# Dealing the last weight sums behind evictions, a spare buffer for one copy, and five smaller moves in a retention + FFN kernel

## The chip, the cores and the metric

The kernel runs on one core of one Trainium2 chip. A core has five engines with a queue each: TensorE (PE, matrix products), VectorE (DVE), ScalarE (ACT), GpSimd (POOL) and SyncE (SP, which here only issues transfers). They run side by side and wait for each other through semaphores. SBUF is the working memory, PSUM [...] the memory that TensorE writes to; moving a result out of PSUM is called an eviction. The metric is the device time of one execution in microseconds, of which the median of several runs is taken.

## The reference

```
# retention: 8 batches, 8 heads, 576 positions, head size 64
scores = (q @ k^T) / sqrt(64)
out    = (scores * D[h]) @ v,   D[h][s, t] = gamma[h] ** (s - t) for s >= t, else 0
x      = out as 4608 tokens x 512
# multiplicative FFN, d_ff = 1024
a, b = x @ w1, x @ w2            # 512 x 1024 each
out  = ((a * b) @ w3) @ w_out    # 1024 x 1024, then 1024 x 512
```

The four weight matrices come as 8-byte floats and are turned into 4-byte floats on the chip.

## The kernel before

**Tokens.** Two batches are treated together, in four pairs. A pair's 576 positions are cut into five chunks (64, then four times 128) for the retention and into three blocks of 192 positions for the FFN; a block holds 384 tokens (two batches), and there are twelve blocks, counted by `m`. The counter `g` runs over the 20 chunks.

**Retention.** For a chunk, `load` fetches k, q, v; `scale` multiplies q and v by the decays (on VectorE, GpSimd or ScalarE); `front` transposes k and q on TensorE (tile `tp`) and ScalarE copies them out (`kT`, `qT`). Later chunks are loaded in 32-blocks and transposed by VectorE instead (`front_blocks`). `score` forms `sc` and VectorE masks it into `pm`; `state` adds to the running state `st`, which ScalarE copies to `sb`; `pv_state` and `pv` form `xps`, and the function that `pv` returns copies it into the block's `xT`.

**FFN, first four blocks (blocks 0 to 3).** `up` computes a and b for one block and one quarter `fp` of the columns with Strassen's seven products (L524). `strassen_tokens` makes the sums of token quarters that these need (L496), `strassen_weights` those of weight quarters (L149). After a product VectorE adds it to a partial sum (`plus`, L529), and behind each such addition `up` issues other work: some steps of the weight conversion (`convert`) and one entry each of the lists `aside` and `spread`. w3 and w_out are multiplied with each other once (`w3_mm`, L477), giving `w3o`; `down` then multiplies the tokens' a*b with `w3o`, again with seven products (L637, tile `po`).

**FFN, the other eight blocks.** Their products (`up2`, L1039) are two-level Strassen products over groups of two blocks. The weight forms for them are made in place in the weight tiles by `weight_forms` (six VectorE sums for each half of the columns and kind, L874), sent to DRAM (`kept`, L884 to L890), and fetched again one step ahead by `next_forms` into a ring of three buffers `ra` (L941), from POOL's queue. `token_forms` builds the sums of tokens as a list `pieces`, of which an entry is issued behind an addition of `down` when `spread` is empty.

**The switch at chunk `g` = 9.** `open_first` takes over the memory of the first half of the weights: it issues the remaining sums of the second half (`spread.extend(weight_forms(1, True))`, `flush()`), whose transfers to `kept` follow them on SP's queue. Then come a product with w_out for blocks 2 and 3, and `open_second`, which closes the PSUM pool `acc` with seven buffers and opens one with five, and a third product with w_out for block 3. In these, `down` copies its first product out of PSUM by ScalarE into `first` (L669): this lies in the output tile `ot` until the ring is in use, and from then on in a spare piece of the ring. `ot` has one buffer, so it is free only when the stores of the product before it have landed.

**What sets the order.** Nothing is scheduled by a planner: each engine takes its instructions in the order in which the Python code issues them. `keep_busy(n)` issues n products of the unit matrix with itself, which no one reads.

Of the kernel before, what the change touches and what calls it, by code (L numbers as in the profile page):

```python
# [19 lines left out]
def kernel(  # L20
# [13 lines left out]
    nc = tc.nc  # L34
# [449 lines left out]
    def has_x(i, n):  # L484
        return any(starts[c] + sizes[c] >= (n + 1) * TB and ("x", i * NC + c) in live for c in range(NC))

    def strassen_tokens(i, n, engine=nc.gpsimd):

        m = every.index((i, n))
        x = live["xT", m]  # L490
        B = [[x[:, 2 * r:2 * r + 2, b, :] for b in range(2)] for r in range(2)]
        T = [(t_first if m == 1 and j == 2 else ffn).tile(
            [P, 2, TB], F32, tag="T", name="T", bufs=1 if m == 1 and j == 2 else 5) for j in range(3)]

        def tt(out, in0, in1, op=ALU.subtract):
            engine.tensor_tensor(out=out, in0=in0, in1=in1, op=op)  # L496

        live["B", i, n] = {"B11": B[0][0], "B21": B[1][0], "B22": B[1][1], "T3": B[0][1],
                           "T1": T[0], "T2": T[1], "-T4": T[2]}
        tt(B[0][1], B[1][1], B[0][1])  # L500
        tt(T[1], B[0][1], B[0][0], ALU.add)
        yield
        tt(T[0], B[1][1], T[1])
        tt(T[2], B[1][0], T[1])
        yield

    def up(i, n, fp, conv=0, tail=True, first=False):
        m = every.index((i, n))
        while ("S", fp) not in live:
            assert go_on() is None  # L510
        if ("B", i, n) not in live:
            list(strassen_tokens(i, n))
        if fp == 0:
            live["ab", i, n] = (pools["ab3"] if m == 2 else ffn).tile([P, 2 * KF, TB], F32, tag="ab", name="ab")
        ab = live["ab", i, n]

        def product(ps, a, b):
            a, b = A(fp, a), live["B", i, n][b]
            new = ps is None
            if new:  # L520
                ps = acc.tile([P, 2, TB], F32, tag="acc", name="up")
            for w in range(2):
                for r in range(2):
                    nc.tensor.matmul(ps[:, w, :], a[:, w, r, :], b[:, r, :], start=(new and w == r == 0),  # L524
                                     stop=(w == r == 1), skip_group_check=True)
            return ps

        def plus(ps, to, sb):
            nc.vector.tensor_add(c[:, to], ps, c[:, sb])  # L529
            convert(conv.pop(0) if isinstance(conv, list) else conv)  # L530
            for extra in (aside, spread):
                if extra:
                    extra.pop(0)()


        c = ffn.tile([P, 4, 2, TB], F32, tag="c", name="c", bufs=1)
        p1 = product(None, "A11", "B11")
        nc.scalar.copy(c[:, 0], p1)

        convert(owed.pop() if owed else 0)  # L540
        if first:

            p7 = product(None, "S3", "T3")
            product(p1, "A12", "B21")
            aside.pop(0)()
        plus(product(None, "S2", "T2"), 1, 0)
        plus(p7 if first else product(None, "S3", "T3"), 2, 1)
        p5 = product(None, "S1", "T1")
        plus(p5, 3, 2)
        plus(product(None, "A22", "-T4"), 2, 2)  # L550
        if not first:
            product(p1, "A12", "B21")
        nc.scalar.copy(c[:, 0], p1)
        product(p5, "S4", "B22")
        plus(p5, 1, 1)

        if fp == NQ - 1 and m < NB - 1 and has_x(*every[m + 1]) and ("B", *every[m + 1]) not in live:
            list(strassen_tokens(*every[m + 1]))
        nc.vector.tensor_mul(ab[:, 4 * fp:4 * fp + 4, :], c[:, :, 0, :], c[:, :, 1, :])
        if tail:  # L560
            convert(conv)
# [63 lines left out]
    def down(x, y, then=None, last=False):  # L625
        a, done, left = pair_of(x, y)
        second = "first" in live
        ahead(x, y)
        while len(done) < (1 if second else 3):
            aside.pop(0)()  # L630
        ps = {}
        ot = pools["ot"].tile([P, 2, 2, DM // 2], F32, tag="ot", name="ot")

        def product(nm, A, B, on=None):
            ps[nm] = ps[on] if on else acc.tile([P, DM // 2], F32, tag="acc", name="po")
            for f in range(NP):
                nc.tensor.matmul(ps[nm], a[A][:, f, :], live["W"][B][:, f, :], start=(f == 0 and not on),  # L637
                                 stop=(f == NP - 1), skip_group_check=True)

        def plus(nm, to, sb):  # L640
            nc.vector.tensor_add(ot[:, to[0], to[1]], ps[nm], ot[:, sb[0], sb[1]])
            if spread:
                spread.pop(0)()
            elif pieces:
                pieces.pop(0)()
            if second and aside and nm != 3:
                aside.pop(0)()

        def put(m, t, row, half=slice(0, 2)):

            i, n = every[m]
            r0 = t * P
            while r0 < (t + 1) * P:
                b = r0 // TB
                e = min((b + 1) * TB, (t + 1) * P)
                r = (2 * i + b) * S + n * TB + r0 - b * TB
                stores.append((out[r:r + e - r0, half.start * DM // 2:half.stop * DM // 2],
                               ot[r0 - t * P:e - t * P, row, half].rearrange("p h d -> p (h d)")))
                r0 = e
            if not keep_stores and not second:  # L660
                store()

        C11, C12, C21, C22 = (0, 0), (0, 1), (1, 0), (1, 1)
        product(1, "A11", "B11")
        first = ot[:, 0, 0]
        if second and steps[0]:
            first = live["first"].pop(0)
            live["first"].append(first)
        nc.scalar.copy(first, ps[1])  # L669
        if second:  # L670
            store()
            finish()
        product(7, "S3", "T3")
        if second:
            multiply()
        while len(done) < 3:
            aside.pop(0)()
        if then:
            ahead(*then)
        product(2, "A12", "B21", on=1)  # L680
        nc.vector.tensor_tensor(out=a["S4"], in0=a["A12"], in1=a["S2"], op=ALU.subtract)
        product(6, "S2", "T2")
        nc.vector.tensor_add(ot[:, 0, 1], ps[6], first)
        nc.scalar.copy(ot[:, 0, 0], ps[2])
        early = second or last or g >= 2 * NC - 1
        if early:
            put(*x, 0, slice(0, 1))
            store()
        plus(7, C21, C12)
        product(5, "S1", "T1")  # L690
        plus(5, C22, C21)
        product(4, "A22", "-T4")
        plus(4, C21, C21)
        put(*y, 1)
        if second:
            store()
        product(3, "S4", "B22", on=5)
        while aside and not early:
            aside.pop(0)()
        plus(3, C12, C12)  # L700
        put(*x, 0, slice(1 if early else 0, 2))
        if last:
            store()
        while aside:
            aside.pop(0)()
# [38 lines left out]
    pv_state(1)  # L744
    convert_up_to(3)
    convert(2)
    state(1)
    load(3, "kq")
    weight_sums = strassen_weights(0)
    next(weight_sums)  # L750
    pv(1)()
    keep_busy(4)
    load(3, "v")
    load_block()
    convert_up_to(4)
# [2 lines left out]
    next(weight_sums)  # L758
    list(token_sums)
    list(weight_sums)  # L760
    aside.append(lambda: scale(2, "q", True))
    scale(2, "v")
    up(0, 0, 0, conv=[0, 0, 2, 2, 2], tail=False, first=True)
    front(2)
    convert(1)
    score(2)
    state(2)
# [143 lines left out]
    def open_first():  # L911
# [3 lines left out]
        ring.append(ra[:, :FORM])  # L915
        next_forms(nc.sync)
        spread.extend(weight_forms(1, True))
        flush()
        free.extend(cs[:, j] for j in range(2))
        live["T2"] = ra[:, FORM:].rearrange("p (s k c t) -> p s k c t", s=2, k=3, c=2)  # L920
        live["E"] = ffn.tile([P, 4, 2, TB], F32, tag="c", name="e", bufs=1).rearrange("p (e r) b t -> p e r b t", e=2)
# [22 lines left out]
    def token_forms(gr):  # L944
# [35 lines left out]
        def inner(k):  # L980
# [5 lines left out]
            for i, nm in enumerate(("T1", "T2") if k != 2 else ("-T4",)):  # L986
                part = [y[:, i] if k != 2 else y for y in (b11, b21, b22, b12, *u)]
                forms[nm] = dict(zip(names, part))

        pieces.extend([first, lambda: tt(b12, b22, b12), lambda: tt(E[:, 1], b12, b11, ALU.add),  # L990
                       lambda: tt(E[:, 0], b22, E[:, 1])])
        pieces.extend([lambda: pair(1), lambda: pair(0), lambda: pair(2), outer, lambda: inner(slice(0, 2)),
                       lambda: inner(2)] if gr else
                      [outer, lambda: pair(1), lambda: pair(0), lambda: pair(2), lambda: inner(slice(0, 2)),
                       lambda: inner(2)])

    behind, results, sums2 = [], [], {}

    def finish():
        while behind:  # L1000
            behind.pop(0)()
# [140 lines left out]
    for g in first_pair:  # L1142
# [9 lines left out]
        if in_blocks[g + 1]:  # L1152
            scale_blocks(g + 1)
            work(n - 1)
            aside.extend(lambda nm=nm: front_blocks(g + 1, nm) for nm in "kq")
            work(1)
            while aside:
                aside.pop(0)()
            half = 0
# [25 lines left out]
    pv(g)()  # L1185
    load(g + 2, "v", nc.scalar)
    load(g + 2, "k")
    scale(g + 1, "v")
    open_first()
    token_forms(0)  # L1190

# [105 lines left out]
```

## Time and profile before

| what | value |
|---|---|
| median of three runs | 838.39 us (836.72 to 839.96) |
| the profiled execution's own time | 944.19 us |
| its span, first to last instruction | 942.5 us |
| mean granted TensorE clock in it | 0.846 |
| busy: PE, DVE, ACT, POOL | 931.7, 545.4, 289.7, 224.4 us |
| chain that ended last | PE 95%, DMA 3%, SP's queue 1% |
| products with w_out, L637 | 26% of the chain |
| products of `up`, L524; of `up2`, L1039 | 18%; 31% (18% and 13%) |
| clock granted from 10 to 15 us / from 30 us on | 0.50 / 0.85 |

The profile shows one execution, and that one took 12.6% longer than the median. Each matrix product of 4-byte floats stands in it as two instructions. "Busy" for PE is modelled: it runs to a modelled end of each product, so a PE that is busy throughout is not necessarily at its peak. A line of the timeline gives the start and the duration of a run of equal instructions, the engine, the source line, the operation, the tiles with their shapes and, in brackets, how long the engine stood idle before it and what released it.

### The profile page before, as it was taken

The numbers are of one execution on the slowest core, as the hardware profiler recorded it, in microseconds if no ns is written. First come the engines' busy times: TensorE is split into PE (matmuls) and PEld (weight loads), VectorE is DVE, ScalarE is ACT, GpSimd is POOL, SyncE is SP. The second block draws the span as 40 slices with busy tenths as digits, with TensorE's granted clock in tenths as the row PEclk, the third lists the DMA queues.
The fourth block names the chain that finished last, engine by engine and source line by source line (L and its number), as shares of the span: only waits on it lengthen the run. The fifth ranks groups of instructions, "written<-read, shape, count | busy, mean of one in ns | idle before, by whom it ended". The sixth has DMA issues, their size and how long they took to land.

```text
span 942.5 us, 15780 instructions
## 1 busy us (share of the span) xinstructions
PE 931.7 (99%) x6101; PEld 818.4 (87%) x6101; DVE 545.4 (58%) x957; ACT 289.7 (31%) x601; POOL 224.4 (24%) x249
## 2 busy tenths in 40 slices
PE   8999999999999999899999999999999999999998
PEld 7999999533888998689999789998789998799976
DVE  4888888970544467644557643657545555535542
ACT  4776454560111111044343023331033320033200
POOL 1100010002003172015536015463016250044500
PEclk7888888888888888888888888888888888888888
DMA  9992543426045475967675146868245352135311
GB/s 187 225 222 74 83 122 98 133 62 99 1 86 111 74 224 197 319 173 194 170 193 154 41 88 207 215 192 160 57 116 192 119 184 73 40 131 187 118 29 40
DMA packets 197868, 126.96 MB, mean 135 GB/s; under 512 B 157848, under 2 KB 179608, under 8 KB 197792
## 3 DMA queue, kind: packets, MB, share of 16 engines
q1 hardware_dynamic: 167520, 50.14, 26.4%
q0 software_dynamic: 11632, 62.79, 20.4%
q10 hardware_dynamic: 18640, 13.02, 5.0%
q8 instruction: 48, 0.79, 0.4%
q14 instruction: 28, 0.23, 0.1%
HBM read 103.62 MB, written 22.28 MB: 134 GB/s over the span
## 4 chain that ended last, share of the span: by engine, by line
PE 95%; DMA 3%; SPq 1%; ACT 0%; POOL 0%; issue 0%; DVE 0%; ACTq 0%
PE po L637 26%; PE up L524 18%; PE up L1039 18%; PE seed L1039 13%; PE ps L477 7%; PE xps L299 4%; PE sc L233 4%; PE xps L274 2%; PE st L255 2%; PE tp L218 1%; DMA ld_v<-in_v_dram 1%; DMA kept<-wA 1%; DMA ld_q<-in_q_dram 1%; DMA out_dram<-ot 1%; SPq L93 0%; SPq L342 0%
## 5 line engine op out<-in xcount | busy, mean ns | idle before, releaser
L637 PE MATMUL po<-w3o,ab 128*128 128x256 f32 x552 | 145.0, 426 | 2.8 <-ACT ot L669 2.2
L637 PEld LDWEIGHTS po<-w3o,ab 128*128 128x128 f32 x552 | 109.4, 200 | 32.5 <-ACT ot L669 2.7
L1044 POOL TENSOR_TENSOR cc<-cc 128x384 f32<-128x384 f32 x112 | 109.3, 1002 | 5.2 <-ACT cc L1062 3.7
L1051 DVE TENSOR_TENSOR cc<-seed,cc 128x384 f32<-128x384 f32 x88 | 49.0, 557 | 91.9 <-PE seed L1039 85.4
L941 POOL DMA_DIRECT2D ra<-kept x53 | 30.0, 566 | 243.5 <-PE seed L1039 181.1
L1039 PE MATMUL up<-xT,ra 128*128 128x192 f32 x384 | 83.7, 360 | 0.0
L529 DVE TENSOR_TENSOR c<-up,c 128x384 f32<-128x384 f32 x80 | 44.0, 551 | 64.9 <-PE up L524 64.4
L524 PE MATMUL up<-xT,wA 128*128 128x192 f32 x384 | 80.5, 360 | 0.0
L637 PE MATMUL po<-wB,forms 128*128 128x256 f32 x288 | 75.8, 425 | 0.0
L524 PEld LDWEIGHTS up<-xT,wA 128*128 128x128 f32 x384 | 72.0, 197 | 1.4 <-issue 0.6
L1051 DVE TENSOR_TENSOR cc<-up,cc 128x384 f32<-128x384 f32 x88 | 48.5, 551 | 42.5 <-PE up L1039 39.8
L1039 PEld LDWEIGHTS up<-xT,ra 128*128 128x128 f32 x384 | 72.0, 198 | 1.3 <-issue 0.4
L637 PEld LDWEIGHTS po<-wB,forms 128*128 128x128 f32 x288 | 57.8, 201 | 15.2
L236 DVE TENSOR_TENSOR pm<-sc,mask 128x512 f32<-128x512 f32 (+1 forms) x80 | 45.4, 627 | 41.2 <-PE sc L233 41.1
L477 PE MATMUL ps<-wo,w3T 128*128 128x512 f32 x128 | 64.4, 673 | 0.0
L1058 ACT COPY seed<-up 128x384 f32<-128x384 f32 x56 | 25.9, 463 | 121.1 <-PE up L1039 118.5
L1039 PE MATMUL up<-ra 128*128 128x192 f32 x288 | 62.5, 359 | 0.0
L477 PEld LDWEIGHTS ps<-wo,w3T 128*128 128x128 f32 x128 | 25.5, 199 | 38.1 <-issue 37.8
L1039 PE MATMUL seed<-e,ra 128*128 128x192 f32 x256 | 57.4, 361 | 0.0
L1039 PEld LDWEIGHTS up<-ra 128*128 128x128 f32 x288 | 54.6, 198 | 0.2
L524 PE MATMUL up<-T,wS 128*128 128x192 f32 x256 | 53.5, 359 | 0.0
L181 POOL TENSOR_TENSOR bl_q<-bl_q,gqs 128x512 f32<-128x512 f32 (+1 forms) x26 | 27.9, 1093 | 103.3 <-DMA bl_q<-in_q_dram 101.3
(126 smaller groups left out, 1550.9 us busy)
## 6 DMA issues: line engine op xcount, KB each, us to landing
ra<-kept POOLq DMA_DIRECT2D x53, 896.0 KB, 4.9
raw<-in_moe_w_dram SPq DMA_DIRECT2D x72, 128.0 KB, 3.1
out_dram<-ot ACTq DMA_DIRECT2D x54, 128.0 KB, 2.3
bl_q<-in_q_dram SPq DMA_DIRECT2D x192, 32.0 KB, 3.0
bl_k<-in_k_dram SPq DMA_DIRECT2D x136, 32.0 KB, 3.0
raw<-in_moe_w_dram SPq DMA_DIRECT2D x16, 256.0 KB, 6.3
ld_k<-in_k_dram SPq DMA_DIRECT2D x8, 512.0 KB, 5.9
raw<-in_moe_w_out_dram SPq DMA_DIRECT2D x32, 128.0 KB, 2.7
```

Source lines behind the costliest of these rows:

```text
L181: nc.gpsimd.tensor_tensor(out=part, in0=part, in1=gqs[:, :, n0:n0 + n].unsqueeze(3).to_broadcast([P, NP, n, BL]), op=ALU.mult)
L233: nc.tensor.matmul(sc[j][:sz, p, :sz], kT[hs, b, p, :sz], qT[hs, b, p, :sz], start=True, stop=True)
L236: nc.vector.tensor_mul(pm[:sz, b, j, :, :sz], sc[j][:sz, :, :sz], mask[:sz, :sz].unsqueeze(1).to_broadcast([sz, NP, sz]))
L299: nc.tensor.matmul(banks[r][heads[half], b, n, :sz], vs[:sz, b * H + 2 * p + j, :], pm[:sz, b, j, p, :sz], start=(c == 0 and m == 0), stop ...
L477: nc.tensor.matmul(ps, live["w3T", ft][:, g, :], live["wo"][:, g, :], start=(g == 0), stop=(g == KF - 1))
L524: nc.tensor.matmul(ps[:, w, :], a[:, w, r, :], b[:, r, :], start=(new and w == r == 0), stop=(w == r == 1), skip_group_check=True)
L529: nc.vector.tensor_add(c[:, to], ps, c[:, sb])
L637: nc.tensor.matmul(ps[nm], a[A][:, f, :], live["W"][B][:, f, :], start=(f == 0 and not on), stop=(f == NP - 1), skip_group_check=True)
L941: engine.dma_start(ring[n % 3], kept[n % 14 // 7][nm])
L1039: nc.tensor.matmul(ps[:, w, :], weight_of(slot, a, w), B[b], start=(new and w == 0), stop=True, skip_group_check=True)
L1044: nc.gpsimd.tensor_tensor(out=o, in0=o, in1=i, op=ALU.add)
L1051: nc.vector.tensor_add(c[:, j], ps, with_add[:, j])
```

## The change

There are seven edits.

1. **Start.** `state(1)` is issued after `pv(1)` and not before it, and `keep_busy(4)` after it becomes `keep_busy(1)`. The transposes of chunk 2 (`front(2)`) move from behind the first `up` into it: those of k behind its third addition, those of q behind its fourth (two empty entries of `aside` stand ahead of them).
2. **Sums of the third block of tokens.** In the `up` for block 1 and the last quarter they are issued on VectorE, one behind each of the first four additions, in place of GpSimd at its end.
3. **Last weight sums.** `open_first` no longer flushes: the three pairs of sums and the transfers stay in `spread` and are issued behind the four additions of the product with w_out of blocks 2 and 3. The token sums of the first group wait until `spread` is empty, and are issued two at a time behind the additions of the product after it.
4. **First copy.** In that next product, `first` lies in the tile `cs` (name `cc`) which `open_first` laid into the first weight half's memory, and no longer in `ot`.
5. **Scaling of v** for chunk 10: on ScalarE, as eight instructions, no longer as one on GpSimd.
6. **Forms.** `down` may issue `next_forms` behind its first copy, so that one transfer per group leaves POOL's queue during a product with w_out and not with the first step of the next group.
7. **Order of VectorE's work.** `front_blocks` for q before k, with an empty place between; and for the later groups the outer token sums before the pairs.

```diff
-    def strassen_tokens(i, n, engine=nc.gpsimd):
+    def strassen_tokens(i, n, engine=nc.gpsimd, singly=False):
...
         tt(B[0][1], B[1][1], B[0][1])
+        if singly:
+            yield
         tt(T[1], B[0][1], B[0][0], ALU.add)
         yield
         tt(T[0], B[1][1], T[1])
+        if singly:
+            yield
         tt(T[2], B[1][0], T[1])
...
+        sums = ()
+        if fp == NQ - 1 and m < NB - 1 and has_x(*every[m + 1]) and ("B", *every[m + 1]) not in live:
+            sums = strassen_tokens(*every[m + 1], nc.vector, True)
+            aside.extend([lambda: next(sums)] * 4)
...
-        if fp == NQ - 1 and m < NB - 1 and has_x(*every[m + 1]) and ("B", *every[m + 1]) not in live:
-            list(strassen_tokens(*every[m + 1]))
+        list(sums)
...
-        if second and steps[0]:
+        if second and not steps[0]:
+            first = live["spare"]
+        elif second:
             first = live["first"].pop(0)
             live["first"].append(first)
         nc.scalar.copy(first, ps[1])
         if second:
             store()
             finish()
+            if steps[0] and sent[0] < steps[0] + 3:
+                next_forms()
...
-    state(1)
     load(3, "kq")
...
     pv(1)()
-    keep_busy(4)
+    state(1)
+    keep_busy(1)
...
-    aside.append(lambda: scale(2, "q", True))
+    aside.extend([lambda: scale(2, "q", True), lambda: None, lambda: None,
+                  lambda: front(2, "k"), lambda: front(2, "q")])
     scale(2, "v")
     up(0, 0, 0, conv=[0, 0, 2, 2, 2], tail=False, first=True)
-    front(2)
...
         spread.extend(weight_forms(1, True))
-        flush()
+        live["spare"] = cs[:, 1].rearrange("p a b t -> p (a b t)")[:, :DM // 2]
...
-        pieces.extend([first, lambda: tt(b12, b22, b12), lambda: tt(E[:, 1], b12, b11, ALU.add),
-                       lambda: tt(E[:, 0], b22, E[:, 1])])
-        pieces.extend([lambda: pair(1), lambda: pair(0), lambda: pair(2), outer, lambda: inner(slice(0, 2)),
-                       lambda: inner(2)] if gr else
-                      [outer, lambda: pair(1), lambda: pair(0), lambda: pair(2), lambda: inner(slice(0, 2)),
-                       lambda: inner(2)])
+        parts = [first, lambda: tt(b12, b22, b12), lambda: tt(E[:, 1], b12, b11, ALU.add),
+                 lambda: tt(E[:, 0], b22, E[:, 1]), outer, lambda: pair(1), lambda: pair(0), lambda: pair(2),
+                 lambda: inner(slice(0, 2)), lambda: inner(2)]
+        if not gr:
+
+            parts = [lambda two=parts[j:j + 2]: [f() for f in two] for j in range(0, 8, 2)] + parts[8:]
+        pieces.extend(parts)
...
-            aside.extend(lambda nm=nm: front_blocks(g + 1, nm) for nm in "kq")
+            aside.extend([lambda: front_blocks(g + 1, "q"), lambda: None, lambda: front_blocks(g + 1, "k")])
...
-    scale(g + 1, "v")
+    scale(g + 1, "v", True)
     open_first()
     token_forms(0)
```

## The prediction

> **What bounds the kernel now.** I read the page first, its busy row and its chain (95% PE), and then measured the starts of successive products against each other.
>
> ```profile
> span 942.5 us, 15780 instructions
> PE 931.7 (99%) x6101; PEld 818.4 (87%) x6101; DVE 545.4 (58%) x957; ACT 289.7 (31%) x601; POOL 224.4 (24%) x249
> ```
>
> TensorE is the bound. Its busy time is modelled, so I took starts: a product of `up` (eight records) starts every 1.50 us, and from 412 us to the end no group of PE's instructions has more than 0.1 us of idle before it. Only idle time of PE can be won. The idle rows and the timeline leave three places. First the start, where a first product waits for a copy:
>
> ```profile
> 25.35 1.21 PE L255 MATMUL st<-ld_v,ld_k 128*64 128x64 f32 x32 [0.28 <-POOL ld_v L204]
> 26.38 2.18 PE L299 MATMUL xps<-pm,ld_v 128*64 128x128 f32 x32
> 28.49 1.27 PE L131 MATMUL idle<-ident 128*128 128x128 f32 x8
> ```
>
> ```profile
> 27.43 0.56 ACT L259 COPY sb<-st 128x512 f32<-128x512 f32 x1
> 28.36 1.07 ACT L306 COPY xT<-xps 128x512 f32<-128x512 f32 x2 [0.36 <-PE xps L299]
> ```
>
> `up` starts at 29.58, when that second copy is out (29.43). Second, a wait of TensorE for VectorE, while GpSimd makes the sums of the third block of tokens:
>
> ```profile
> 122.56 1.50 DVE L413 SCALAR_TENSOR_TENSOR e<-raw,e 128x512 int32<-128x512 int32 x1
> ...
> 125.17 1.09 DVE L399 TENSOR_SCALAR m<-raw 128x512 int32<-128x512 int32 x1
> ...
> 126.66 1.30 DVE L402 SCALAR_TENSOR_TENSOR m<-raw,m 128x512 f32<-128x512 uint32 x1
> ```
>
> ```profile
> 128.48 1.74 PE L524 MATMUL up<-xT,wS 128*128 128x192 f32 x8 [0.65 <-DVE c L529]
> ```
>
> Elsewhere these three take 0.68, 0.42 and 0.69 us. Third, the switch of pools:
>
> ```profile
> 391.07 4.25 PE L637 MATMUL po<-w3o,ab 128*128 128x256 f32 x16 [0.52 <-DVE ot L641]
> 397.49 3.19 PE L637 MATMUL po<-w3o,ab 128*128 128x256 f32 x8 [2.16 <-ACT ot L669]
> ```
>
> ```profile
> 397.06 0.37 ACT L669 COPY ot<-po 128x256 f32<-128x256 f32 x1 [11.59 <-DMA kept<-wA]
> ```
>
> ```profile
> 395.00:400.00 5.00, 2.84 (x9) 2.06 (x8) 0.00 (x0) 0.37 (x1) 0.00 (x0) 0.73 1.11 372
> ```
>
> The last is the view by windows: the seventh figure (0.73) is the granted clock, 0.85 around it. So after the wait the clock is lower, here and from 400 to 405 (0.73 again): 10 x 0.12 / 0.85 = 1.4 us more.
>
> **What the skill says.** The Trainium skill, "SBUF — State Buffer", section "Who interferes with whom", has VectorE and GpSimd share a pair of ports: an instruction of VectorE with two SBUF inputs blocks against a GpSimd instruction that reads SBUF. The trace agrees for the sums: 0.82 + 0.67 + 0.61 = 2.1 us lost over three instructions beside GpSimd's four. (The middle one has one tensor input, which that sentence does not cover.) "TensorE: Matmul & The Clock Gate", section "What's actually happening", halves the clock after a window of some 3.4 us with too little work, and the window runs freely. The trace agrees: 1.4 us are what 3.4 us at 0.5 in place of 0.85 cost, after an idle time of only 2.2 us. So it needn't trip in every execution.
>
> **The time frame.** The profiled execution took 944.19 us against a median of 838.39, a ratio of 0.89. At a clock of 0.846 TensorE's work would shrink to 797 us at full clock, so the runs shown are probably at a faster clock, with more waiting than the profile has. Waits on copies, transfers and VectorE don't shrink. I make the sum in the profile's frame and then look at what 0.89 does to PE's share.
>
> **Part by part.**
>
> *Start.* Before, `st` holds PE from 25.35 to 26.38 and `xps` till 28.5. After, `xps` comes first: v is ready at 25.3 and the last mask product of VectorE at 25.43 (22.95 + 2.48), so it ends near 27.5. ScalarE is free at 27.5 and has no `sb` copy ahead: copies out at 28.55. `st` ends at 28.5, one idle product adds 0.3: `up` at 28.7, 0.85 earlier. The second product needs VectorE's token sum, issued at 29.68 in a stream without a gap since 25.35, ready at 30.23; the first takes 1.5 us, so it just fits. Three idle products (0.3 us each) were filling, not work. The moved transposes cost PE the same 1.0 us each, and their copies come earlier on ScalarE, in the place of an eviction whose user is VectorE at 42. Gain 0.85; nothing if VectorE's stream holds it back later, 1.2 if the 0.18 us before the next scores goes too.
>
> *Third block.* Added to VectorE: four sums at 0.5 us (0.55, 0.56, 1.02 for two, L496 at 29.7) = 2.1 us, in the `up` from 130.06 to 140.60, where its idle times are 0.17 + 0.19 + 2.11 = 2.5 us: hidden. If that cover is gone they cost up to 2.1 us. Taken away: the 2.1 us of blocking just before. The wait of 0.65 us falls. Their user starts at 140.6; the last sum is issued behind the fourth addition, near 137. Gain 0.65; ends -1.0 and +2.1.
>
> *Last weight sums.* Before, six sums ran in a row (377.02 to 383.04) while products went on, hiding all. After, they sit behind the additions of a product, as the pairs before them already do:
>
> ```profile
> 367.63 0.42 DVE L641 TENSOR_TENSOR ot<-po,ot 128x256 f32<-128x256 f32 x1
> 367.97 1.22 DVE L874 TENSOR_TENSOR wA<-wA 128x1024 f32<-128x1024 f32 x1
> 369.10 0.95 DVE L874 TENSOR_TENSOR wS<-wS 128x768 f32<-128x768 f32 x1
> 369.97 0.42 DVE L641 TENSOR_TENSOR ot<-po,ot 128x256 f32<-128x256 f32 x1
> ```
>
> Every addition then takes 2.34 us against 2.03 of a product. That product began at 358.79; its last addition ended at 375.06, 16.27 us on, while PE needs 14.24. The product with the same pattern is now the one in front of `open_second`, whose first product waits for just that last addition. The wait there grows from 0.67 (start to start) to some 2.05 us, with all of PE's queue behind it: a new loss of 1.4 us.
>
> *First copy.* With `cc` it no longer waits for the stores of the product before; `cc` needs the transfers out of the first half's sums, issued by 383. The wait of 2.35 us (start to start) goes: the next writers of `ot`, VectorE's L683 and ScalarE's L684, come some 6 us after the stores' issue, which took 5.7 to land. Behind L684 stand a store and the scaling of q (2.44 us), whose transposes start 8 us later. Net at the switch 3.0 before, 2.05 after: gain 0.95. The lowered clock may stay, as one wait of 2 us is much like the one that brought it: I take half of 1.4. Together 1.65; ends 0 and 2.4.
>
> *Transfers.* SP's sends for the second half stood at 388.18; they now follow the third pair, near 392.2. Queued behind them: the next fetch into the ring (402.62, then 406.6), landing in about 5.3, so 412 at the usual time, 415 at the slowest (8.2); its step starts near 416. ScalarE's own fetch (410.81) waits for the same sends. Taken at nothing; it is the loss of the second rival.
>
> *v on ScalarE.* Eight at 0.305 us = 2.44 ahead of the copy of the first product, which then ends near 380.0; its user starts at 380.37. Hidden, by 0.4; at the faster clock a loss up to 0.2. GpSimd's 1.9 us were on nobody's path.
>
> *Forms, order of transposes, order of sums.* PE has no idle in these stretches. A fetch needs 4.9 us, and even before it was issued two steps of 5.3 us ahead; its 0.57 us on POOL now stand before `scale_blocks`, whose user is a chunk away. VectorE is busy about 23 of 40 us there. Nothing; ends -0.5 and +0.5.
>
> *Sum.* 0.85 + 0.65 + 1.65 = 3.15 of 942.5 (0.33%). At 0.89, the start gives some 0.7; at the switch products of 1.8 us make the new wait 2.7 and the old ones 3.5, 0.8 gained. So about 2.9 us off 838.4: 835.5.
>
> **The rivals.** *Larger gain.* From 40 to 200 us VectorE is busy 136.7 of 160 us; at a faster clock PE would need 142, and VectorE is nearly the bound. Then whatever unblocks it counts fully: 1.2 + 2.1, with the switch at 0.95 and a clock that no longer drops, 1.4: 5.65, 832.7. For it: the waits that 838 must contain. Against: four sums are added where 2.1 us are freed.
>
> *A late fetch, slower.* The transfer engines are full (a share of 1.0 to 1.2 from 375 to 400 us). I have the sends landed at 406.6; from 410.7 on the fetch behind them (5.3 us) is later than its step at 416, and ScalarE stands at its own fetch with the first evictions of the next stage behind it. Sends at 414 and the slowest fetch (8.2) make PE stand 6 us, and the clock drops (1.4); less the 3 gained: 843. Against: four us of slack.
>
> *No effect.* VectorE's stream absorbs the start, the clock drops as before: 838.
>
> **Numbers.** Forecast 0.36, no effect 0.11 (both within 0.5%, 4.2 us, about what a measurement of this kernel can tell from no change), larger gain 0.34, slower 0.19. The forecast's own range is 834 to 837.5; 830 to 842 takes in most of the larger gain and part of the loss.
>
> **What would show it.** `up` at 28.7; no wait for VectorE near 128 and L399, L402, L413 at usual lengths; at the switch one wait of 2 us for L648 (the addition, renumbered), none for the first copy; the clock there. Wrong if PE waits on `ra` after the switch, or if the gain lies in the later groups.

## The result, and the profile after

| | median, us | ratio to before (95% interval) |
|---|---|---|
| before | 839.34 (835.90 to 843.75) | 1 |
| after | 840.27 (836.12 to 843.99) | 1.0005 (0.9989 to 1.0022) |

The change makes no difference that the measurement can tell: +0.4 us, between -0.9 and +1.8. The forecast was 835.5. The prediction read a profile of before at a mean clock of 0.846, and after's is at 0.998, so times are compared below only with a second profile of before, at 0.994 (span 834.6 us), called "before, second profile".

The page of after, its busy row:

```profile
span 839.2 us, 15778 instructions
PE 819.8 (98%) x6095; PEld 738.9 (88%) x6095; DVE 542.3 (65%) x961; ACT 291.9 (35%) x609; POOL 216.6 (26%) x244
```

TensorE is busy 820 us and not 932; what the change can win or lose is in the 19 us beside that, and in the clock. The timeline of after, the three places that the prediction named. First the start:

```profile
28.09 1.47 PE L528 MATMUL up<-xT,wA 128*128 128x192 f32 x8
30.35 1.86 PE L528 MATMUL up<-xT,wA 128*128 128x192 f32 x10 [0.80 <-DVE xT L496]
...
54.94 1.38 PE L528 MATMUL up<-T,wS 128*128 128x192 f32 x7 [1.22 <-ACT e L395]
```

In before's second profile the first two of these read:

```profile
29.29 1.47 PE L524 MATMUL up<-xT,wA 128*128 128x192 f32 x8
30.96 2.84 PE L524 MATMUL up<-xT,wA 128*128 128x192 f32 x16 [0.21 <-DVE xT L496]
```

`up` starts early as forecast, but its second product waits 0.80 us for VectorE's token sum, as it does for 0.21 us in before. Ahead of the edit, at the first scores, after is 0.62 us earlier already (21.74 against 22.36). The first product is 1.20 us earlier, so the edit won some 0.6; the token sum (29.66 against 30.27) and the second product are 0.61 earlier, so nothing of it is left there. At 54.94 one product waits 1.22 us, where before's waits 0.65. (ScalarE is named there, but the sum of weights that this product reads is made by VectorE from 54.11 to 54.80, the second of four in a row without a gap: VectorE is what is full.) Second, near 118 us, no wait of over 0.3 us is left. Third, the switch:

```profile
350.34 5.45 PE L644 MATMUL po<-w3o,ab 128*128 128x256 f32 x24 [2.68 <-DVE ot L648]
...
352.37 0.37 ACT L678 COPY cc<-po 128x256 f32<-128x256 f32 x1 [9.14 <-PE po L644]
```

The addition (L641 of before) is late by 2.68 us, the figure that the prediction has for a faster clock. The first copy waits only for its product. So far this is as forecast. The surprise stands 24 us later, in the first steps of `up2`. First TensorE, then ScalarE, then SP's queue:

```profile
369.78 0.81 PE L1051 MATMUL up<-xT,ra 128*128 128x192 f32 x4
374.67 0.92 PE L1051 MATMUL up<-xT,ra 128*128 128x192 f32 x4 [4.08 <-ACT cc L1074]
```

```profile
368.51 0.46 ACT L1070 COPY seed<-up 128x384 f32<-128x384 f32 x1 [2.61 <-PE up L1051]
373.76 0.34 ACTq L723 DMA_DIRECT2D out_dram<-ot  x1
374.14 0.48 ACT L1074 COPY cc<-up 128x384 f32<-128x384 f32 x1 [5.17 <-DMA bl_q<-in_q_dram]
```

```profile
362.80 0.34 SPq L952 DMA_DIRECT2D ra<-kept  x1
363.19 0.43 SPq L93 DMA_DIRECT2D ld_q<-in_q_dram  x1
364.01 14.43 SPq L171 DMA_DIRECT2D bl_q<-in_q_dram  x13
```

After the copy of `seed` (L1070) ScalarE's next instruction is the issue of a store of the output tile (L723). It goes out at 373.76, 4.8 us later, and the copy into `cc` that TensorE needs is behind it. What releases ScalarE is the landing of a block load of q, which has nothing to do with the output. After the wait the clock is low; the view by windows, whose seventh figure is the granted clock:

```profile
376.00:380.00 4.00, 4.00 (x16) 4.00 (x16) 2.52 (x5) 1.57 (x5) 0.00 (x0) 0.61 0.41 64
```

Why a load of q holds back a store is in the trace, which names the semaphore that each transfer counts up when it lands. In after the 591 transfers of SP's and ScalarE's queues use eight of these counters, handed out in turn. In the 510 cases where the trace has the landing of a counter's last user, none of the next users was issued before it. The store's counter is semaphore 102, which the first of the block loads of q has too: that load has landed at 373.68, the wait of ScalarE's queue for 102 ends at 373.72, and the store goes out at 373.76. Which transfer had the counter last depends on the transfers of both queues in between. (The fetches into the ring at the switch leave from these two queues, and not from POOL's.) For this store:

```
kernel                       its counter was last used by
before, second profile       the fetch ra<-kept on SP's queue, landed 1.2 us before the store's turn
first copy alone             the same fetch, landed when ScalarE had stood 2.6 us at the store
changed                      the first of sixteen block loads bl_q on SP's queue
sums in a row; switch alone  an earlier store of the output, landed 2.5 and 0.7 us before its turn
```

The Trainium skill, "DMA: Bandwidth & Descriptors", section "Why a DMA increments its semaphore by 16 and not by 1", says why a program would wait so: with two transfers in flight on one semaphore, a count can be reached before the first has fully landed. It advises a semaphore for each slot in flight. No run here tries two transfers on one counter; that a store waits for the landing of an unrelated transfer is what the trace shows, 4.8 us long.

### The profile page after: what moved, and what is told of

Read it like the earlier page. It is cut to its first block, busy times and chain, and to the rows that moved or that the text cites. A ratio compares the mean times of both kernels' runs of the same rounds, so it can differ in the third digit from the quotient of the medians.

```text
span 839.2 us, 15778 instructions
## 1 busy us (share of the span) xinstructions
PE 819.8 (98%) x6095; PEld 738.9 (88%) x6095; DVE 542.3 (65%) x961; ACT 291.9 (35%) x609; POOL 216.6 (26%) x244
## 4 chain that ended last, share of the span: by engine, by line
PE 81%; DMA 7%; DVE 4%; issue 2%; SPq 2%; ACT 1%; POOL 1%; ACTq 0%; DVEq 0%; POOLq 0%
PE po L644 22%; PE up L1051 17%; PE up L528 13%; PE seed L1051 13%; PE ps L477 7%; PE sc L233 3%; PE xps L299 3%; PE xps L274 2%; DMA ld_v<-in_v_dram 1%; PE st L255 1%; DMA bl_q<-in_q_dram 1%; SPq L171 1%; DMA ra<-kept 1%; PE tp L218 1%; DMA raw<-in_moe_w_dram 1%
## 5 line engine op out<-in xcount | busy, mean ns | idle before, releaser
L644 PE MATMUL po<-w3o,ab 128*128 128x256 f32 x552 | 125.1, 381 | 4.0 <-DVE ot L648 3.2
L1051 PE MATMUL up<-xT,ra 128*128 128x192 f32 x384 | 74.5, 330 | 6.0 <-ACT cc L1074 4.1
L528 PE MATMUL up<-xT,wA 128*128 128x192 f32 x384 | 70.7, 328 | 0.8 <-DVE xT L496 0.8
L1051 PEld LDWEIGHTS up<-xT,ra 128*128 128x128 f32 x384 | 64.3, 191 | 7.5 <-ACT cc L1074 4.4
L528 PEld LDWEIGHTS up<-xT,wA 128*128 128x128 f32 x384 | 63.3, 190 | 2.2 <-PE up L528 1.1
L644 PE MATMUL po<-wB,forms 128*128 128x256 f32 x288 | 65.1, 379 | 0.0
L1070 ACT COPY seed<-up 128x384 f32<-128x384 f32 x56 | 25.9, 463 | 102.7 <-PE up L1051 62.0
L477 PE MATMUL ps<-wo,w3T 128*128 128x512 f32 x128 | 55.1, 592 | 0.0
L1051 PE MATMUL up<-ra 128*128 128x192 f32 x288 | 54.8, 326 | 0.0
L1051 PEld LDWEIGHTS up<-ra 128*128 128x128 f32 x288 | 48.1, 190 | 0.1
L528 PE MATMUL up<-T,wS 128*128 128x192 f32 x256 | 46.8, 326 | 1.2 <-ACT e L395 1.2
```

Source lines behind the costliest of these rows:

```text
L477: nc.tensor.matmul(ps, live["w3T", ft][:, g, :], live["wo"][:, g, :], start=(g == 0), stop=(g == KF - 1))
L1051: nc.tensor.matmul(ps[:, w, :], weight_of(slot, a, w), B[b], start=(new and w == 0), stop=True, skip_group_check=True)
L1070: nc.scalar.copy(p6, p1)
```

## The experiments

Two theories. **A**: the forecast gains are real and are paid back by two new waits at the switch, 2.7 us for the addition and 4.1 us for ScalarE at its store. **B**: at full clock VectorE absorbs the gains, and the two waits stand in both kernels. Differences in us below are (ratio - 1) x 839.

To compare profiles by stage I took, for each kernel, the starts of the same products in it and in the second profile of before. The difference is the lag, and its growth over a stretch is what that stretch costs. In us, negative is gained; the positions are those of before's second profile, whose own row is zero:

| kernel | 21 to 55 | 100 to 138 | 236 to 308 | 308 to 335 | 345 to 351.5 | 351.5 to 358 | 367 to 380 |
|---|---|---|---|---|---|---|---|
| after | +0.3 | -0.83 | -1.98 | 0.0 | +2.35 | -1.62 | +6.07 |
| sums in a row | +0.7 | -0.83 | -1.97 | 0.0 | 0.0 | -1.62 | +3.97 |
| store by GpSimd | +0.9 | -0.85 | -1.95 | 0.0 | +2.34 | +0.07 | 0.0 |
| v first | +0.2 | -0.83 | -1.97 | 0.0 | 0.0 | -1.61 | 0.0 |
| v first, old start | +0.7 | -0.83 | -1.97 | 0.0 | 0.0 | -1.62 | 0.0 |
| switch alone | +0.3 | 0.0 | +0.1 | 0.0 | +2.34 | +0.07 | 0.0 |
| start alone | +2.0 | 0.0 | -0.2 | +0.8 | +0.1 | +3.27 | 0.0 |
| third block alone | +2.2 | -0.80 | -0.5 | 0.0 | 0.0 | +1.82 | 0.0 |
| order alone | +2.2 | 0.0 | -1.98 | +1.4 | 0.0 | +0.76 | 0.0 |
| v on ScalarE alone | +0.6 | 0.0 | +0.8 | 0.0 | 0.0 | +1.60 | 0.0 |
| first copy alone | +0.7 | 0.0 | +0.3 | 0.0 | 0.0 | -1.62 | +2.86 |
| first copy, freed | +0.9 | 0.0 | +0.1 | 0.0 | +0.2 | -1.62 | +0.62 |

The columns leave out stretches in between. The largest of these holds a wait of TensorE for a fetch into the ring near 550 us. It stands in every one of these profiles, before's second one too (1.69 us there, 1.88 in after, 0.4 to 3.0 in all), and moves the lag by -1.3 to +2.9 from 500 to 600 us, +0.25 in after. It follows no edit that I can see.

**Before, unchanged, second profile** (836.31 us). The kernel before as it is.

> The kernel before, unchanged, for a second profile: the one shown was taken at a mean granted clock of 0.846, the one of the changed kernel at 0.998. Theory A (the gains are real, and are paid back at the switch of pools by two new waits: 2.7 us for VectorE's addition before the first product of `open_second`, 4.1 us for ScalarE, which stands at a store): the two profiles at full clock differ by little in their sum; before has here waits of some 0.65 us for VectorE near the third block, about 0.6 for the addition at the switch, 2.4 or more for the first copy, and none of over 0.5 us for ScalarE in the first steps of `up2`. Theory B (at full clock VectorE's stream absorbs the early gains, and the two waits of the switch are there in both kernels): the same 2.7 and 4.1 us stand in before as well, and `up` starts early in the changed kernel without its second half being earlier.

Its timeline has the wait of the third block, two of the same kind that the slow profile did not have, and the switch:

```profile
119.50 1.57 PE L524 MATMUL up<-xT,wS 128*128 128x192 f32 x8 [1.15 <-DVE c L529]
...
290.65 1.57 PE L524 MATMUL up<-xT,wS 128*128 128x192 f32 x8 [0.65 <-DVE c L529]
...
306.86 1.57 PE L524 MATMUL up<-xT,wS 128*128 128x192 f32 x8 [0.79 <-DVE c L529]
...
350.91 3.72 PE L637 MATMUL po<-w3o,ab 128*128 128x256 f32 x16 [0.52 <-DVE ot L641]
355.97 1.99 PE L637 MATMUL po<-w3o,ab 128*128 128x256 f32 x8 [1.35 <-ACT ot L669]
```

The 2.7 and 4.1 us are not there, and B falls. This execution is a short one: its first copy waits 1.35 us, where the other four kernels that keep the old copy lose 0.8 to 3.3 us more in that column.

**Sums in a row.** The changed kernel with edit 3 undone.

```diff
         spread.extend(weight_forms(1, True))
+        flush()
         live["spare"] = cs[:, 1].rearrange("p a b t -> p (a b t)")[:, :DM // 2]
...
-        if not gr:
-
-            parts = [lambda two=parts[j:j + 2]: [f() for f in two] for j in range(0, 8, 2)] + parts[8:]
```

> The changed kernel with the last weight sums again in a row before the switch, and the sums of the third block's tokens one by one as before; the first copy still goes to the spare buffer. Theory A: the addition before `open_second`'s first product is no longer late (wait 2.7 falls to 0.7 or less), and the store in the first step of `up2` no longer stands (4.1 falls to under 0.5), since the transfers that it is behind are sent earlier: 5 to 7 us less than the changed kernel, 833 to 835. Theory B: the waits move to the first product after the sums; no more than 1 us less, 839 to 841.

834.66 us, ratio 0.994 (0.9919 to 0.9961): 5.0 us faster than before, 5.4 less than the changed kernel. Both waits go (0.52 at the addition, none at the store), as A has it. Of the 6.07 us of the last column 3.97 remain, by a wait that nobody forecast:

```profile
372.99 1.18 PE L1049 MATMUL seed<-e,ra 128*128 128x192 f32 x4 [1.98 <-ACT seed L1068]
...
370.93 1.28 ACT L202 ACTIVATE ld_q<-ld_q,gq 128x128 f32<-128x128 f32 x4 [3.24 <-DMA ld_q<-in_q_dram]
```

TensorE is now 4.5 us ahead, and ScalarE's scaling of q comes before its load has landed.

**Store by GpSimd.** The changed kernel with this one store in another queue, nothing else.

```diff
-    def store():
+    def store(engine=nc.scalar):
...
-            nc.scalar.dma_start(*stores.pop(0))
+            engine.dma_start(*stores.pop(0))
...
-        store()
+        store(nc.gpsimd if steps[0] == 1 else nc.scalar)
```

> The changed kernel with one store moved: the last quarter of the output before the switch, issued in the first step of `up2`, goes through GpSimd's queue in place of ScalarE's. Nothing else moves. Theory A (ScalarE stands at the issue of this store, which waits for an unrelated transfer of SP's queue to land, with the evictions of `up2` behind it): the wait of 4.1 us for ScalarE's copy into `cc` goes, and the low clock after it: 4 to 5.8 us less than the changed kernel, 834.5 to 836. Theory B (the evictions are late because of the load that ScalarE's queue is said to wait for, or because the product itself is late): unchanged within 1 us.

836.95 us, ratio 0.9972 (0.9959 to 0.9985): 2.8 less than the changed kernel by the ratios, 1.0 to 4.5 by their two intervals. The last column falls from +6.07 to 0. It is less than the 4 to 5.8 expected; in this profile the clock dropped after the wait for the addition, which cost back 1.69 us (+0.07 in place of -1.62), and whether that happens oftener than in the changed kernel one profile of each can't tell. That the store is what holds ScalarE is shown; that its wait is 4.1 us in most executions of the changed kernel is not.

**Switch alone.** The kernel before with edits 3 and 4, and the order of the token sums of edit 7.

```diff
-        flush()
+        live["spare"] = cs[:, 1].rearrange("p a b t -> p (a b t)")[:, :DM // 2]
...
-        if second and steps[0]:
+        if second and not steps[0]:
+            first = live["spare"]
+        elif second:
...
+            parts = [lambda two=parts[j:j + 2]: [f() for f in two] for j in range(0, 8, 2)] + parts[8:]
```

> The kernel before with two parts of the change alone: the last weight sums dealt behind evictions, and the first copy in the spare buffer. Theory A: the wait for the addition (2.7 us) is here too, the first copy waits for nothing (2.4 to 3.5 us less), and the store of the first step of `up2` stands behind an old store and not behind the loads, so that the 4.1 us do not come: within 1 us of the kernel before, 838 to 840, and 0 to 1 us faster rather than slower. If the 4.1 us come here too, they belong to these two parts, and the sum is 3 to 5 us slower than before, 842 to 844. Theory B: as before within 0.5 us, with both waits in the profile of before.

839.49 us, ratio 1.0007 (0.9993 to 1.002). As A says: a wait of 2.7 us for the addition, none for the copy, no stand at the store, whose counter was free. The two edits cancel.

**First copy alone.** The same without the part on the sums.

> The kernel before with the first copy in the spare buffer alone; the last weight sums stay in a row ahead of the switch. The wait for the first copy was 1.5, 3.2, 3.3 and 2.3 us in the four profiles of kernels that have the old copy, with the clock low for some 3 us after it in two of them. Theory A (the two parts at the switch cancel: the copy wins what the late addition loses): 2.6 us faster than before, up to 1.7 more by the clock: 835 to 836.5, and 3 to 4 us under the run that has the dealt sums too. Theory B (the copy's wait hides behind another, so that nothing is won): 838 to 839, with a new wait where the removed one stood.

838.33 us, ratio 0.9995 (0.9977 to 1.0014): not the 2.6 us of A. The copy's wait is gone (-1.62 where kernels with the old copy have 0 to +3.3), and the gain is lost 20 us on, at the same store. Its counter is the one of before, but TensorE comes 1.6 us earlier here and the fetch into the ring lands at 372.48, not 368.99:

```profile
373.46 0.92 PE L1042 MATMUL up<-xT,ra 128*128 128x192 f32 x4 [1.94 <-ACT cc L1065]
...
372.55 0.34 ACTq L714 DMA_DIRECT2D out_dram<-ot  x1
372.93 0.48 ACT L1065 COPY cc<-up 128x384 f32<-128x384 f32 x1 [3.02 <-DMA ra<-kept]
```

(The expectation has the clock low behind the old copy's wait in two of its four profiles. It is so in one, the start alone.)

**First copy, freed.** That kernel with the store by GpSimd, and with half of a scaling of v ahead of the scaling of q.

```diff
+                beside.append(lambda: scale(g + 1, "v", range(H // 2)))
                 beside.extend(lambda j=j: scale(g + 1, "q", range(j, j + H // 2)) for j in (0, H // 2))
...
-            beside.extend(lambda j=j: scale(g + 1, "v", range(j, j + H // 2)) for j in (0, H // 2))
+            beside.extend(lambda j=j: scale(g + 1, "v", range(j, j + H // 2))
+                          for j in ((0, H // 2) if q_blocks else (H // 2,)))
```

> The run with the first copy alone (838.33), with the two waits taken away that its profile shows 20 us after the switch: ScalarE's store in the first step of `up2` goes through GpSimd's queue (TensorE waited 1.9 us there for the copy behind it, ScalarE 3.0 us until a fetch of SP's queue had landed), and half of a scaling of v goes ahead of the scaling of q, which stood 1.5 us for its load and cost TensorE 0.4. If the copy's win was passed on to these two waits: 2.3 to 3 us less, 835.3 to 836, and no wait of over 0.5 us from 345 to 380 us but the addition's 0.52. If the win is lost elsewhere: 838, with a wait in the next fetch into the ring or in the copies of q.

836.21 us, ratio 0.9971 (0.9959 to 0.9984): 2.4 faster than before, 2.0 less than without the two edits. The last column falls from +2.86 to +0.62. The copy's win was passed on, and is had once ScalarE stands nowhere behind it. The two edits on the kernel before without the first copy were not run; in before's second profile no wait of TensorE over 0.2 us from 358 to 380 is there for them to remove.

**Start alone, third block alone, order alone, v on ScalarE alone.** Edits 1, 2, the half of 7 that concerns `front_blocks`, and 5, each on the kernel before, as in the diff of the change.

> The kernel before with one part of the change alone: the state's products behind the first products of p v, one idle product in place of four, the transposes of the third chunk dealt. The prediction's step Start gave it 0.7 us. By the two traces at full clock the first product of `up` comes about 1 us earlier, and only some 0.3 us of it are left at 55 us, since VectorE's sum of tokens and the copies of the next scores are then late instead. Theory A: 0.2 to 0.7 us faster, 838.7 to 839.2. Theory B (VectorE's stream takes all of it): 0, 839.4.

> The kernel before with one part of the change alone: the four sums of the third block of tokens by VectorE. The prediction's step Third block gave 0.65 us, with ends of -1.0 and +2.1. The traces at full clock show 1.3 us gained at 118 us and some 0.5 given back by 138. Theory A: 0.8 us faster, 838 to 839, and the wait for VectorE at 118 us gone while those near 290 and 306 stay. Theory B (VectorE is full there and takes it back): 0, with waits for VectorE at 130 to 138 of the length of the one removed.

> The kernel before with one part of the change alone: VectorE's transposes of the blocks of q and k in the order q, nothing, k. The prediction took it at nothing, with ends of -0.5 and +0.5. The traces at full clock show 0.8 us less at 290 us and 1.1 us less at 306 us in every kernel that has this part with others. If it is this part: 1.5 to 2 us faster, 837.4 to 838, no wait for VectorE at 290 us, and L874's two sums near 301 us at 1.5 and 1.0 us in place of 2.5 and 1.8, since GpSimd's scaling of the blocks of q comes behind them. If these come from the other parts: 839.4, waits as before.

> The kernel before with one scaling of v, ahead of the switch, on ScalarE in place of GpSimd. The prediction said that GpSimd's 1.9 us there were on nobody's path. In two of four profiles with GpSimd's scaling one weight sum of VectorE that ran beside it took 2.6 us in place of 1.2, and TensorE waited 0.9 to 1.3 us for the addition behind it, near 333 us. If that is a loss of the kernel before: 0.5 to 1.3 us faster, 837.7 to 838.5, with no such wait. If not: 839, or 0.2 slower by the first copy of that product.

| alone | median, us | ratio (95% interval) |
|---|---|---|
| start | 840.17 | 1.0018 (1.0003 to 1.0033) |
| third block | 837.57 | 0.9983 (0.9964 to 1.0001) |
| order | 837.25 | 0.9983 (0.9969 to 0.9997) |
| v on ScalarE | 839.52 | 1.0006 (0.9990 to 1.0021) |

The *third block* gains 0.8 in each of the six profiles that have it; its own run is 1.4 faster, but its interval (3.0 faster to 0.1 slower) takes in no change. The *order* gains 2.0 us in all six, and its run is faster by 1.4 (0.3 to 2.6). The view is the timeline, VectorE's and then GpSimd's, of before (second profile) and then of after:

```profile
301.45 2.50 DVE L874 TENSOR_TENSOR wA<-wA 128x1024 f32<-128x1024 f32 x1
303.87 1.80 DVE L874 TENSOR_TENSOR wS<-wS 128x768 f32<-128x768 f32 x1
...
302.83 3.76 POOL L181 TENSOR_TENSOR bl_q<-bl_q,gqs 128x512 f32<-128x512 f32 x2
```

```profile
299.39 1.50 DVE L885 TENSOR_TENSOR wA<-wA 128x1024 f32<-128x1024 f32 x1
300.82 0.95 DVE L885 TENSOR_TENSOR wS<-wS 128x768 f32<-128x768 f32 x1
...
302.57 2.07 POOL L181 TENSOR_TENSOR bl_q<-bl_q,gqs 128x512 f32<-128x512 f32 x2 [2.76 <-DMA bl_q<-in_q_dram]
```

In before GpSimd's scaling of the blocks of q runs beside VectorE's sums, and these take 2.50 and 1.80 us; TensorE waits for the addition behind them (306.86 above). In after the scaling waits 2.76 us for the last blocks of q, and by then the sums are over. Why these land later, the queues of before (second profile) and then of after tell:

```profile
288.60 8.55 SPq L171 DMA_DIRECT2D bl_q<-in_q_dram  x16
295.29 0.40 ACTq L93 DMA_DIRECT2D ld_v<-in_v_dram  x1
```

```profile
293.23 0.44 ACTq L93 DMA_DIRECT2D ld_v<-in_v_dram  x1
...
297.80 1.79 SPq L171 DMA_DIRECT2D bl_q<-in_q_dram  x4
```

It is the counters again. The sixteen loads begin earlier in after (285.65), but the thirteenth has the counter that ScalarE's load of v had last, and goes out at 297.80, when v has landed (297.78). In before v's load takes its counter later in the turn, all sixteen are out by 297, and it holds back a load of k (300.85, v landed at 300.83). It is so in all six kernels with the new order and in none of the seven without; the second of the two sums takes 0.95 us in all six and 1.80 or more in all seven. No run separates the counter from the order itself. What the sums lose is the blocking of the Trainium skill's "SBUF — State Buffer", section "Who interferes with whom": 1.22 and 0.95 us undisturbed at the switch. The other gain of this edit, the wait at 290.65, has another cause: in before VectorE stands 1.85 us for the blocks of k (till 287.32), with q's transpose and the additions behind it, and one of these came too late for the product. In after q's blocks, which are there, are transposed first, at 284.25.

*v on ScalarE* moves nothing measurable: the wait that it removes stands in two of the seven profiles with the old scaling (+0.8 and +1.4), and in its own run the first copy waited long, +1.60. The *start* alone is slower by 1.5 us (0.3 to 2.8). In its profile TensorE waits 6.5 us for the first loads of q, against 2.2 in before's second one, all of it before the edit acts; but that is one execution, the longest of its 22 (844.51), and the reason is not shown.

**v first.** The kernel with the sums in a row, and with the same edit on the scaling of v as above.

> The changed kernel with the last weight sums again in a row before the switch, and with half of a scaling of v put ahead of the two halves of the scaling of q on ScalarE in the first three steps of `up2`. In the run without that second edit ScalarE stood 3.2 us for the load of q, TensorE 2.0 us behind it, and the clock was low for some 3 us after it (1.4). If this wait alone is taken away: 3.4 us less than that run's 834.66, 831 to 832. If the wait moves to the next fetch into the ring (0.4 us there in that run): 832.5 to 834.5.

831.89 us, ratio 0.9925 (0.9912 to 0.9939): 6.3 us faster than before, the lowest median of all. The wait for q's scaling is gone. The profile is of the longest of its six executions (834.67), and has the longest wait of all for a fetch into the ring near 549 us (in the view of waits: total, times, longest):

```profile
PE up L1049 <- DMA ra<-kept: 3.0, 1, 3.0
```

That this edit made it grow is not shown: it is 0.4 us in the sums in a row, but 1.5 in the next run and 2.2 in the first copy, freed.

**v first, old start.** That kernel with edit 1 undone.

> The run at 831.89 (sums in a row, half of v ahead of q) with the start of the kernel before: the state's products ahead, four idle products, the transposes of the third chunk after the first `up`. If the new start loses 1.2 us, as its run alone says: 830.7. If it gains the 0.3 us that the traces show at 55 us: 832.2. If the 1.2 us came from the loads at the start, which vary from run to run by more than that: between, 831.5 to 832.5.

832.76 us, ratio 0.9921 (0.9892 to 0.9949). By medians the new start is 0.9 better here, by the ratios 0.3 worse, and both lie within the interval; the run of the start alone says worse. What it is worth stays open.

## Why the prediction was right or wrong

By its own steps; sizes from the table of lags.

- **Start**, 0.85 (0.7). This step failed. `up` was early (28.09), and what the edit won was lost at the next product. From 21 to 55 us five profiles with the new start lose 0.2 to 2.0 (mean 0.8), eight with the old one 0 to 2.2 (mean 1.0). The step named this end ("nothing if VectorE's stream holds it back later") and chose the other. "It just fits" was worked out at a lower clock, where the first product covers the wait; at full clock before's second product already waits 0.21 us for VectorE's token sum, so an earlier first product could win nothing.
- **Third block**, 0.65. Right: 0.83, which is 1.3 won at 118 us less 0.5 given back by 138.
- **Last weight sums**, a loss of 1.4, or a wait of 2.7 at a faster clock. Right: 2.68 measured, 2.35 more than before.
- **First copy**, -2.35. The wait goes, and is worth about 3.1: 1.62 against before's second profile, in which it was short, and 1.5 more as the mean of the five kernels with the old copy (0, 3.27, 1.82, 0.76, 1.60). The half of 1.4 for the clock was neither right nor wrong. With a wait of 2.68 us at the switch the clock dropped in two of three profiles, at 1.7 us each; in after it dropped behind the wait at 374 instead, where 6.07 - 4.1 leaves 2.0, of which the clock explains 1.7.
- **Transfers**, "taken at nothing". This step failed. SP's sends ended at 358.96 and ScalarE's own fetch went out at 364.69, so what the step looked at was on time. It asked which buffers the transfers wait for, and left out that a transfer also waits for its counter, and that dealing the sums changes which transfer that is. In after's profile the price was 4.08 us of TensorE and 2.0 us behind it, 1.7 of these by the low clock; in the timed runs the store alone is worth 2.8 (1.0 to 4.5).
- **Forms, order of transposes, order of sums**, "nothing; ends -0.5 and +0.5". It failed the other way, by 2.0 us. "PE has no idle in these stretches" was read from a profile in which a product of `up` takes 1.50 us; at 1.30 the waits of 0.65 and 0.79 us come out. Here too the counters were left out, and this time they helped. Edit 6 was not run alone.
- **v on ScalarE**: "on nobody's path" was wrong in two of seven profiles, too little to measure.

So the sum for after, against an average execution of before: third block -0.8, order -2.0, first copy -3.1, v about -0.3, start about -0.2, together -6.4; the addition +2.35, the store +6.1: +2.0. With the 2.8 of the timed runs for the store the sum is -1.3. The measured +0.4 (-0.9 to +1.8) lies between; the sum is no closer than that, since the term of the store comes from one profile and that of the first copy from few. The rival *A late fetch, slower* had the engine, the place and nearly the size: ScalarE stands "with the first evictions of the next stage behind it", 4.1 + 2.0 us against its 6 + 1.4. Its cause, SP's late sends, was another. *Larger gain*, 832.7, is near where the kernel comes out once the two waits are gone: 834.66, and 831.89 with v first. That is luck in the main: its 1.2 for the start is not there, its 2.1 for the third block is 0.8, and the first copy (3.1) and the order (2.0) make up for it.

## What to carry to other kernels

Waits must be looked for in a profile at the clock at which the kernel is timed: at 0.846 two waits of TensorE for VectorE (0.65 and 0.79 us at full clock) and that for the ring near 550 us (1.69) were hidden, and a third was 0.65 and not 1.15. Where an edit adds, removes or shifts transfers, look at every later transfer issue on an engine that also evicts: it can stand for a transfer that shares only its counter, and all evictions stand behind it; and a load can be late for the same reason. Where a wait is taken out, the next transfer is needed by as much earlier: the win of the first copy came back as a wait at the store, and that of the sums in a row as one for the load of q.

## What was not expected of the hardware

A low clock after a wait that is shorter than the window. The Trainium skill, "TensorE: Matmul & The Clock Gate", section "What's actually happening", has the clock halve after an idle window of some 3.4 us, and has the window run freely. The traces agree on the window: behind each of the waits below the clock stands at 0.50 for 3.41 us, which takes 1.7 us from TensorE. They differ on "idle", and the measurement decides. I cut each of the thirteen profiles at full clock, from some 22 us on, into windows of 3.413 us that begin where the clock record has its steps (3088 windows), and summed TensorE's idle time, as the profile models it, in each. The clock dropped behind all nine windows with 1.97 us of idle time or more, and behind none of those with 1.86 or less; of the two in between, that with 1.92 dropped and that with 1.94 did not. So in these profiles some 1.9 us in one window are enough.

That is why waits of one length cost differently. The 2.68 us at the switch fell into two windows in after, with 1.94 us of idle time in the fuller one, and cost nothing more; in the store by GpSimd and in the switch alone 2.07 and 2.52 us fell into one, and cost 1.7 us more. A wait of 3.17 us in the third block alone was cut into 1.31 and 1.86, and the clock held. Where the windows fall differs from profile to profile, so a wait of 2 to 3 us costs the clock in some executions only; one of 4.08 us puts at least 2.04 us into one window wherever it falls.
